# Where the first decay rows, the first block of k and its cast are queued in an attention-then-MLP kernel

## The chip, the cores and the metric

The kernel runs on one core of a Trainium2 chip. The metric is the device time of one execution in microseconds (us); the median of three runs of the kernel before is 340.68 us. The core has five engines that run their own instruction streams in order: TensorE (PE in the profile, its weight loads PEld), VectorE (DVE), ScalarE (ACT), GpSimd (POOL) and SyncE (SP), which here only issues transfers. ScalarE and GpSimd issue transfers as well. An engine waits for another through semaphores.

## The reference

Eight sequences of 576 positions with 8 heads of 64 go through causal attention with a decay: the scores get the difference of cumulated logarithms of a forget gate f. The result goes through an MLP of 512 to 2048 to 512 whose activation is h - tanh(h).

```python
scores = q @ k.T / sqrt(64)
cum = cumsum(log(clip(f, 1e-4, 1)))            # along the sequence
scores = where(causal, -1e9, scores + cum[i] - cum[j])
x = softmax(scores) @ v                        # heads side by side: 4608 x 512
h = x @ w_in                                   # 4608 x 2048
out = (h - tanh(h)) @ w_out                    # 4608 x 512
```

Inputs and output are float32. The kernel computes with 16-bit floats (f16) and sums in float32.

## The kernel before, in words

**Attention.** TensorE needs q and k with the head dimension on the partitions. For batch 0 they are loaded in five blocks of 128 positions (the last of 64) into `qa` and `ka`, with the positions on the partitions, 8 heads side by side and 68 columns a head. Columns 0 to 63 hold q or k; the others hold the decay, in such a way that one matmul over 67 rows gives score plus decay. A constant, -1 or 1, stands in the other side's column, so the columns are preset by memsets (L138 to L140). TensorE then turns each block by multiplying with an identity matrix `id16` (`quarter0`, L283, for four heads of q or of k; `trans0`, L297, for four heads of both, in one PSUM tile `t`), and VectorE or ScalarE copies the turned block into `QT` and `KT` (L286, L288, L308, L310). `half0` is `trans0` with both of its copies. `scores0` makes the scores of a block (L325, and L328 adds the causal mask), and ScalarE takes the exponential (L330). `values0` multiplies with v, `norm0` divides, `turn0` turns the result for the MLP.

**Decay.** The rows of f for all 64 heads lie in `lf` (a part of the tile `snap`) and are loaded in two parts, columns 0 to 255 and 256 to 575. `logs` clips each part on VectorE (L157) and takes the logarithm on ScalarE (L159). `decay_sum` cumulates on VectorE (L173); its first part is called only after both clips stand in VectorE's stream. `decay_turn` turns eight rows of the sums for batch 0 on TensorE into the PSUM tile `ct` (L192), and `decay_cols` writes them into the decay columns of `qa` and `ka` (L197 to L200).

**The first block of k.** k of block 0 is loaded as float32 by SyncE into `k0`, which borrows the space of the MLP's second weights (so the profile calls it `wout`, L124), and VectorE casts it into `ka` (L692). All the other loads of q, k, v and of the weights are issued by GpSimd, which casts them to f16 on the way (L94, L98, L105, L204, L208, L212). They use eight semaphores in turn, so from the ninth on GpSimd waits for the landing of the load eight places earlier before it issues the next.

**Order.** The order on every engine is the order of the program text; nothing is reordered. The head of the kernel is written out by hand: loads, then `spin(8)`, eight matmuls without use, then the decay sums, the turns and the scores of block 0, and so on. From batch 1 on, the work goes in slots: one slot holds the attention of two heads of one batch (`scores` L384, `values` L412, then a DMA turns the result, L427 and L429), with the loads for later batches and MLP steps put between by `slot`. How many MLP steps a slot takes stands in the list `TAKE`, whose first entry is for slot 4. What is left after the last slot runs at the end.

**MLP.** A step is about 0.9 us of TensorE: `mlp1` makes 512 columns of h (L474 for the first unit of 512 rows, L488 for the others), of which ScalarE takes the tanh (L440) and VectorE the difference (L441). For the first unit `mlp2` multiplies with the second weights (L609); the other units use a scheme with seven half-size products (`seven`, L529), for which VectorE adds up blocks (L455).

Of the kernel before, what the change touches and what calls it, by code (L numbers as in the profile page):

```python
# [8 lines left out]
FP32 = mybir.dt.float32  # L9
FP16 = mybir.dt.float16  # L10
# [12 lines left out]
def kernel(  # L23
# [10 lines left out]
    nc = tc.nc  # L34
    P = 128

    B, H, S, D = q.shape
# [5 lines left out]
    NJ = 5  # L43
    AW = D + 4
# [6 lines left out]
    UW = 512  # L51
# [13 lines left out]
    ps_tr = ctx.enter_context(tc.tile_pool(name="ps_tr", bufs=1, space=PSUM))  # L65
    ps_m = ctx.enter_context(tc.tile_pool(name="ps_m", bufs=3, space=PSUM))
# [10 lines left out]
    HH = H // 2  # L77
    raw = [[qkp.tile([P, RW], FP16, tag=f"{x}n{i}", name=f"{x}n{i}") for i in range(2)] for x in "qk"]
    qn, kn = ([t[0:S // NT6, :].rearrange("p (h n d) -> p h n d", h=H, n=NT6) for t in ts] for ts in raw)
    qa, ka = (t[0][:, 0:NJ * H * AW].rearrange("p (n h d) -> p n h d", n=NJ, h=H) for t in raw)  # L80
# [33 lines left out]
    def load_v(b, n):  # L114
# [5 lines left out]
    lf, cum = (x[0:NH, :] for x in snap)  # L120
    frows = f.rearrange("b h s -> (b h) s")
    nc.scalar.dma_start(out=lf[:, 0:2 * P], in_=frows[:, 0:2 * P])
    k0 = wout[:, 0:2, :].bitcast(FP32).rearrange("p a (h d) -> p (a h) d", d=D)
    nc.sync.dma_start(out=k0, in_=k[0, :, 0:P, :].rearrange("h p d -> p h d"))  # L124
    nc.scalar.dma_start(out=lf[:, 2 * P:S], in_=frows[:, 2 * P:S])
    id16 = cst.tile([P, P], FP16)
    id32 = cst.tile([H, H], FP32)
    neg16 = cst.tile([P, P], FP16)
# [6 lines left out]
    cq = cst.tile([NH, S], FP16)  # L135
    EL = [cst.tile([P, 192], FP16, tag=f"el{i}", name=f"el{i}") for i in range(3)]
    nc.vector.memset(one128, 1.0)
    nc.gpsimd.memset(qa[:, 0, :, D:AW], -1.0)  # L138
    nc.vector.memset(qa[:, 1:NJ, :, D:AW], -1.0)
    nc.vector.memset(ka[:, :, :, D + 2:AW], 1.0)  # L140
    nc.vector.memset(ones16, 1.0)
    nc.vector.memset(id16, 0.0)
# [5 lines left out]
    load_first(ka, k, 1)  # L148
    nc.gpsimd.affine_select(out=tri16, in_=tri16, compare_op=ALU.is_ge,
                            fill=BIG, base=0, pattern=[[1, P]], channel_multiplier=-1)  # L150
    nc.vector.memset(vn[0][:, :, :, D:VW], 1.0)
    nc.vector.memset(vn[0][D:P, NJ - 1, :, 0:D], 0.0)
    nc.vector.memset(KT[0][:, :, S:PITCH], 0.0)
# [18 lines left out]
    def decay_sum(c0, c1):  # L172
        nc.vector.tensor_tensor_scan(out=cum[:, c0:c1], data0=ones16[0:NH, c0:c1], data1=lf[:, c0:c1],  # L173
                                     initial=cum[:, c0 - 1:c0] if c0 else 0.0, op0=ALU.mult, op1=ALU.add)
# [12 lines left out]
    def decay_turn(blocks):  # L187
        if not CT:
            CT.append(ps_tr.tile([P, UW], FP32, tag="tr", name="ct"))
        for ib in blocks:  # L190
            t0 = min(ib * P, S - P)
            nc.tensor.transpose(out=CT[0][:, ib * H:(ib + 1) * H], in_=cum[0:H, t0:t0 + P], identity=id32)  # L192
# [38 lines left out]
    for b in range(2, B):  # L231
        p0 = (b - 1) * NPAIR
# [20 lines left out]
    def spin(n):  # L253
        av = ps_av.tile([P, 2, 512], FP32, tag="av", name="spin")
        for _ in range(n):
            nc.tensor.matmul(out=av[:, 0, :].rearrange("p (a n) -> p a n", n=P), lhsT=one128[:, 0, :],
                             rhs=one128.to_broadcast([P, UW // P, P]))
# [21 lines left out]
    def quarter0(ib, a, x, eng):  # L279
        t32 = ps_m.tile([P, UW], FP32, tag="m", name="t32")  # L280
        t16 = t32.bitcast(FP16)[0:D + 3, 0:HH * P].rearrange("p (h n) -> p h n", h=HH)
        for h in range(HH):
            nc.tensor.transpose(out=t16[:, h, :], in_=(qa, ka)[x][:, ib, a * HH + h, 0:D + 3], identity=id16)  # L283
        to = (QT, KT)[x][0][:, a * HH:(a + 1) * HH, ib * P:(ib + 1) * P]
        if eng == "A":
            nc.scalar.activation(out=to, in_=t16, func=AF.Copy)  # L286
        else:
            nc.vector.tensor_copy(out=to, in_=t16)  # L288

    def trans0(ib, a, pool, engs):  # L290
        p0 = max(0, (ib + 1) * P - S)
        pn = P - p0
        t32 = pool.tile([P, UW], FP32, tag="tr" if pool is ps_tr else "m", name="t32")
        t16 = t32.bitcast(FP16)[0:D + 3, 0:H * pn].rearrange("p (x h n) -> p x h n", x=2, h=HH)
        for x, src in enumerate((qa, ka)):
            for h in range(HH):
                nc.tensor.transpose(out=t16[:, x, h, :], in_=src[p0:P, ib, a * HH + h, 0:D + 3],  # L297
                                    identity=id16[p0:P, p0:P])
        T0[(ib, a)] = t16, engs

    T0 = {}

    def copy0(ib, a, x):
        w = min(P, S - ib * P)
        t16, engs = T0[(ib, a)]
        to = (QT, KT)[x][0][:, a * HH:(a + 1) * HH, ib * P:ib * P + w]
        if engs[x] == "A":
            nc.scalar.activation(out=to, in_=t16[:, x, :, :], func=AF.Copy)  # L308
        else:
            nc.vector.tensor_copy(out=to, in_=t16[:, x, :, :])  # L310

    def half0(ib, a, pool, engs):
        trans0(ib, a, pool, engs)
        copy0(ib, a, 0)
        copy0(ib, a, 1)
# [343 lines left out]
    def slot(p, take):  # L659
        items = att_items(p)  # L660
        whole, n, base = sum(c != "" for _, c in items), 0, goal[0]
        for i, (emit, what) in enumerate(items):
            emit()
            if take in FEW and p < 2 * NPAIR:
                if what in FEW[take] and not (what == "s1" and p > NPAIR) or what == "v":
                    step()
                continue
            n += what != ""
            upto(base + n * take // whole)
        goal[0] = base + take  # L670
        upto(goal[0])
# [17 lines left out]
    load_qk(kn, k, 1, 2, HH)  # L689
    spin(8)  # L690
    decay_sum(0, 2 * P)
    nc.vector.tensor_copy(out=ka[:, 0, :, 0:D], in_=k0)  # L692
    decay_turn((0, 1))
    decay_cols(0, 2)
    decay_sum(2 * P, S)
    nc.vector.tensor_scalar_mul(out=neg16, in0=id16, scalar1=-BIG)
    spin(1)
    quarter0(0, 0, 0, "V")
    quarter0(0, 0, 1, "A")
    half0(0, 1, ps_m, "VV")  # L700
    decay_turn((2, 3, 4))
    scores0(0, 0)
    decay_cols(2, NJ)
# [80 lines left out]
    norm0(4)  # L784
    step()
    goal[0] = done[0]
    TAKE = [4, 4, 5, 5, 7, 9] + [8, 8, 7, 8, 8, 7, 7] + 4 * [8, 8, 7, 7]
    for p in range(NPAIR, len(pairs) + 1):
        slot(p, TAKE[p - NPAIR])
        if p == NPAIR:  # L790
# [30 lines left out]
```

## Time and profile before

| | |
|---|---|
| median of three runs (340.52 to 342.07) | 340.68 us |
| the profiled execution, its own time | 341.17 us |
| span in its profile | 339.4 us |
| TensorE busy | 330.8 us, 97% |
| VectorE busy | 240.7 us, 71% |
| ScalarE busy | 227.2 us, 67% |
| GpSimd busy | 163.3 us, 48% |
| read from and written to memory | 36.85 and 9.44 MB |

The span runs from the program's first to its last instruction; the execution's own time is 1.8 us longer. A line of the profile that names an operation gives the engine, the line of the program, the tiles written and read (`out<-in`), the shape, and in brackets how long the engine was idle before it and what ended that. Matmuls are pipelined, so a TensorE that is shown as busy is not always at its peak.

### The profile page before, as it was taken

The numbers are of one execution on the slowest core, as the hardware profiler recorded it, in microseconds if no ns is written. First come the engines' busy times: TensorE is split into PE (matmuls) and PEld (weight loads), VectorE is DVE, ScalarE is ACT, GpSimd is POOL, SyncE is SP. The second block draws the span as 40 slices with busy tenths as digits, with TensorE's granted clock in tenths as the row PEclk, the third lists the DMA queues.
The fourth block names the chain that finished last, engine by engine and source line by source line (L and its number), as shares of the span: only waits on it lengthen the run. The fifth ranks groups of instructions, "written<-read, shape, count | busy, mean of one in ns | idle before, by whom it ended". The sixth has DMA issues, their size and how long they took to land.

```text
span 339.4 us, 8811 instructions
## 1 busy us (share of the span) xinstructions
PE 330.8 (97%) x3404; PEld 238.8 (70%) x3404; DVE 240.7 (71%) x491; ACT 227.2 (67%) x425; POOL 163.3 (48%) x324
## 2 busy tenths in 40 slices
PE   6999999999999999999999999999999999999995
PEld 3888876655588458888885578656877786486484
DVE  6688785649995886478845885588548874974973
ACT  4687887778856886588657875787568734624731
POOL 8958459851978627772776277633322210000000
PEclk9899999999999999999999999999999999999999
DMA  9999999999999999999999999998220022002002
GB/s 118 151 191 171 195 198 150 156 164 212 184 156 143 188 206 136 150 228 199 122 148 233 167 141 164 180 198 178 58 97 19 20 66 95 1 33 93 2 31 93
DMA packets 162955, 46.09 MB, mean 136 GB/s; under 512 B 141602, under 2 KB 162402, under 8 KB 162914
## 3 DMA queue, kind: packets, MB, share of 16 engines
q0 software_dynamic: 100208, 18.23, 81.6%
q1 hardware_dynamic: 62546, 27.17, 40.2%
q8 instruction: 26, 0.43, 0.5%
q10 hardware_dynamic: 160, 0.15, 0.1%
q14 instruction: 15, 0.12, 0.1%
HBM read 36.85 MB, written 9.44 MB: 136 GB/s over the span
## 4 chain that ended last, share of the span: by engine, by line
PE 90%; DVE 4%; ACT 3%; DMA 1%; issue 1%; ACTq 0%
PE hps L488 30%; PE cx L529 17%; PE cz L529 12%; PE ps L384 11%; PE av L412 7%; PE ops L609 4%; PE hps L474 3%; PE ps L325 2%; DVE gt L441 1%; PE t L297 1%; DMA snap<-in_f_dram 1%; PE av L340 1%; ACT e L330 1%; PE t L268 1%; ACT e L393 1%
## 5 line engine op out<-in xcount | busy, mean ns | idle before, releaser
L441 DVE TENSOR_TENSOR gt<-hps,th 128x512 f16<-128x512 f32 x144 | 98.8, 688 | 46.0 <-ACT th L440 45.2
L488 PE MATMUL hps<-XR,win 128*128 128x512 f16 (+4 forms) x640 | 125.7, 336 | 0.0
L393 ACT ACTIVATE e<-ps 128x512 f16<-128x512 f32 x168 | 98.3, 595 | 35.0 <-PE ps L384 30.9
L440 ACT ACTIVATE th<-hps 128x512 f32<-128x512 f32 x144 | 86.1, 598 | 27.8 <-PE hps L488 17.1
L403 POOL TENSOR_SCALAR_AFFINE_SELECT e<-e 128x128 f16<-128x128 f16 x162 | 57.3, 354 | 98.3 <-ACT e L393 97.9
L488 PEld LDWEIGHTS <-win 128*128 128x128 f16 x640 | 56.0, 97 | 43.3 <-issue 0.3
L384 PE MATMUL ps<-QT,KT 67*128 67x512 f16 (+1 forms) x336 | 68.3, 277 | 0.3 <-ACT e L393 0.3
L529 PEld LDWEIGHTS <-gt 128*128 128x128 f16 x640 | 60.5, 97 | 10.3 <-DVE gt L441 0.4
L384 PEld LDWEIGHTS <-KT 67*128 67x128 f16 x336 | 32.1, 98 | 18.4 <-issue 0.7
L94 POOL DMA_DIRECT2D vn<-in_v_dram x40 | 34.5, 863 | 5.7 <-DMA win<-in_moe_w_in_dram 3.1
L529 PE MATMUL cz<-wout,gt 128*128 128x256 f16 x256 | 32.4, 272 | 0.0
L412 PEld LDWEIGHTS <-e 128*128 128x128 f16 x784 | 27.9, 97 | 3.5
L412 PE MATMUL av<-vn,e 128*128 128x65 f16 x784 | 29.1, 193 | 0.0
L529 PEld LDWEIGHTS <-sw 128*128 128x128 f16 x256 | 23.7, 97 | 3.7
L522 DVE TENSOR_TENSOR snap<-cz,snap 128x512 f32<-128x512 f32 x24 | 16.5, 689 | 13.7 <-PE cz L529 6.0
L529 PE MATMUL cx<-kn,gt 128*128 128x256 f16 x192 | 25.2, 272 | 0.0
L420 DVE TENSOR_TENSOR xn<-av,rs 128x640 f16<-128x640 f32 x28 | 23.1, 825 | 1.0
L105 POOL DMA_DIRECT2D kn<-in_k_dram x25 | 21.3, 853 | 1.0 <-issue 1.0
L105 POOL DMA_DIRECT2D qn<-in_q_dram x25 | 21.3, 851 | 1.0 <-issue 1.0
L330 ACT ACTIVATE e<-ps 128x512 f16<-128x512 f32 x25 | 14.4, 595 | 4.3 <-PE ps L328 3.0
L474 PE MATMUL hps<-XR,win 128*128 128x256 f16 x128 | 16.6, 272 | 0.3 <-DVE gt L441 0.3
L566 ACT ACTIVATE snap<-cx 128x512 f32<-128x512 f32 (+1 forms) x18 | 9.9, 550 | 10.4 <-PE cx L529 10.4
(114 smaller groups left out, 377.3 us busy)
## 6 DMA issues: line engine op xcount, KB each, us to landing
vn<-in_v_dram POOLq DMA_DIRECT2D x32, 128.0 KB, 6.9
out_dram<-snap SPq DMA_DIRECT2D x16, 256.0 KB
qn<-in_q_dram POOLq DMA_DIRECT2D x24, 128.0 KB, 6.8
kn<-in_k_dram POOLq DMA_DIRECT2D x23, 128.0 KB, 5.1
QT<-TQ SPq DMA_DIRECT2D x10, 288.0 KB
KT<-TK SPq DMA_DIRECT2D x10, 288.0 KB
out_dram<-ost SPq DMA_DIRECT2D x11, 256.0 KB
win<-in_moe_w_in_dram POOLq DMA_DIRECT2D x4, 512.0 KB, 8.8
```

What stands on the lines that cost most here:

```text
L94: nc.gpsimd.dma_start(out=dst[0:pn, n, h0:h1, 0:D], in_=src[b, h0:h1, n * P:n * P + pn, :].rearrange("h p d -> p h d"))
L105: nc.gpsimd.dma_start(out=to, in_=src[b, :, n * P:n * P + pn, :].rearrange("h p d -> p h d"))
L384: nc.tensor.matmul(out=ps[:, col:col + n], lhsT=KT[b % 2][0:D + 3, h, j * P:(j + 1) * P], rhs=QT[b % 2][0:D + 3, h, i0:i0 + n], start=True ...
L393: nc.scalar.activation(out=e[:, lo:hi], in_=ps[:, lo:hi], func=AF.Exp, scale=qscale)
L403: nc.gpsimd.affine_select(out=view, in_=view, compare_op=ALU.is_ge, fill=0.0, base=0, pattern=pat, channel_multiplier=-1)
L412: nc.tensor.matmul(out=av[:, a, ib, :], lhsT=E.pop((b, 2 * c + a, j, ib)), rhs=vn[b % 2][:, j, 2 * c + a, 0:D + 1], start=(j == 0), stop=( ...
L420: nc.vector.tensor_tensor(out=xn.rearrange("p i (a d) -> p a i d", a=2), in0=av[:, :, :, 0:D], in1=rs.to_broadcast([P, 2, NJ, D]), op=ALU. ...
L440: nc.scalar.activation(out=th, in_=hps, func=AF.Tanh, scale=-1.0)
L441: nc.vector.tensor_tensor(out=to, in0=view(hps), in1=view(th), op=ALU.add)
L474: nc.tensor.matmul(out=hps[:, w * SB:(w + 1) * SB], lhsT=win[:, ci, ft * P:(ft + 1) * P], rhs=XR[:, ci, t * SB:(t + 1) * SB], start=(ci == ...
L488: nc.tensor.matmul(out=hps[:, o:o + n], lhsT=win[:, ci, ft * P:(ft + 1) * P], rhs=XR[:, ci, t:t + n], start=(ci == 0), stop=(ci == NCH - 1))
L529: nc.tensor.matmul(out=ps, lhsT=stationary(u, LHS[ph], ft, m), rhs=moving(RHS[ph], ft), start=fresh and ft == 0, stop=(ft == HF - 1), skip ...
```

## The change

Four things are moved:

- The second part of the decay rows is issued by SyncE, as its first transfer, and not by ScalarE behind the first part. The float32 k of block 0 follows it on SyncE.
- The cast of that k runs on GpSimd, behind the third load and the second mask, and ahead of the loads of block 2. VectorE no longer does it. In exchange VectorE presets all of q's extra columns, block 0's included.
- `trans0` can turn q alone or k alone. In block 0, the second half of q is turned directly behind the first half of q, and then come the two halves of k. The copies are the same.
- Slot 14 takes seven MLP steps and not eight; each later step runs one place later, and one more runs at the end.

```diff
     nc.scalar.dma_start(out=lf[:, 0:2 * P], in_=frows[:, 0:2 * P])
     k0 = wout[:, 0:2, :].bitcast(FP32).rearrange("p a (h d) -> p (a h) d", d=D)
+    nc.sync.dma_start(out=lf[:, 2 * P:S], in_=frows[:, 2 * P:S])
     nc.sync.dma_start(out=k0, in_=k[0, :, 0:P, :].rearrange("h p d -> p h d"))
-    nc.scalar.dma_start(out=lf[:, 2 * P:S], in_=frows[:, 2 * P:S])
...
-    nc.gpsimd.memset(qa[:, 0, :, D:AW], -1.0)
-    nc.vector.memset(qa[:, 1:NJ, :, D:AW], -1.0)
+    nc.vector.memset(qa[:, :, :, D:AW], -1.0)
...
     nc.gpsimd.affine_select(out=tri16, in_=tri16, compare_op=ALU.is_ge,
                             fill=BIG, base=0, pattern=[[1, P]], channel_multiplier=-1)
+    nc.gpsimd.tensor_copy(out=ka[:, 0, :, 0:D], in_=k0)
...
-    def trans0(ib, a, pool, engs):
+    def trans0(ib, a, pool, engs, xs=(0, 1)):
         p0 = max(0, (ib + 1) * P - S)
         pn = P - p0
...
-        for x, src in enumerate((qa, ka)):
+        if 0 in xs:
+            t32 = pool.tile([P, UW], FP32, tag="tr" if pool is ps_tr else "m", name="t32")
+            t16 = t32.bitcast(FP16)[0:D + 3, 0:H * pn].rearrange("p (x h n) -> p x h n", x=2, h=HH)
+            T0[(ib, a)] = t16, engs
+        t16 = T0[(ib, a)][0]
+        for x in xs:
...
     decay_sum(0, 2 * P)
-    nc.vector.tensor_copy(out=ka[:, 0, :, 0:D], in_=k0)
     decay_turn((0, 1))
...
     quarter0(0, 0, 0, "V")
+    trans0(0, 1, ps_m, "VV", (0,))
     quarter0(0, 0, 1, "A")
-    half0(0, 1, ps_m, "VV")
+    trans0(0, 1, ps_m, "VV", (1,))
+    copy0(0, 1, 0)
+    copy0(0, 1, 1)
...
-    TAKE = [4, 4, 5, 5, 7, 9] + [8, 8, 7, 8, 8, 7, 7] + 4 * [8, 8, 7, 7]
+    TAKE = [4, 4, 5, 5, 7, 9] + [8, 8, 7, 8, 7, 7, 7] + 4 * [8, 8, 7, 7]
```

More of the change, by code (lines that the diff above doesn't have):

```diff
@@ L288, in quarter0 @@
             nc.vector.tensor_copy(out=to, in_=t16)
-    def trans0(ib, a, pool, engs):
+    def trans0(ib, a, pool, engs, xs=(0, 1)):
         p0 = max(0, (ib + 1) * P - S)
         pn = P - p0
-        t32 = pool.tile([P, UW], FP32, tag="tr" if pool is ps_tr else "m", name="t32")
-        t16 = t32.bitcast(FP16)[0:D + 3, 0:H * pn].rearrange("p (x h n) -> p x h n", x=2, h=HH)
-        for x, src in enumerate((qa, ka)):
+        if 0 in xs:
[4 more added lines that the diff above has]
+        for x in xs:
             for h in range(HH):
-                nc.tensor.transpose(out=t16[:, x, h, :], in_=src[p0:P, ib, a * HH + h, 0:D + 3],
+                nc.tensor.transpose(out=t16[:, x, h, :], in_=(qa, ka)[x][p0:P, ib, a * HH + h, 0:D + 3],
                                     identity=id16[p0:P, p0:P])
-        T0[(ib, a)] = t16, engs
     T0 = {}
```

## The prediction

> **What bounds the kernel now.** I read the page's busy times first, then the busy time by stage, then who waited for whom on TensorE, then the chain of work over the first 12 us, and last the engines' own timelines there.
>
> ```profile
> PE 330.8 (97%) x3404; PEld 238.8 (70%) x3404; DVE 240.7 (71%) x491; ACT 227.2 (67%) x425; POOL 163.3 (48%) x324
> ...
> 100.00:150.00 50.00, 50.00 (x525) 36.76 (x523) 33.77 (x68) 34.41 (x67) 33.03 (x63) 1.00 1.71 173
> ...
> PE ct L192 <- DVE snap L173: 2.1, 1, 2.1
> ...
> PE ps L325 <- ACT e L330: 1.0, 3, 0.4
> ```
>
> The stage rows (stretch, its length, then PE, PEld, DVE, ACT, POOL busy, clock, DMA) show TensorE busy in all of a stretch of 50 us at full clock, and the page in 97% of the span. The longest of its few waits, 2.1 us, is for the sum of the decay rows. So whatever makes TensorE's first turns start earlier is carried to the end, unless something later is not ready for an earlier TensorE.
>
> ```profile
> 0.82 0.55 ACTq L122
> 1.40 3.79 DMA snap<-in_f_dram
> 5.21 0.58 DVE snap L157
> 5.86 0.60 DVE snap L173
> 6.51 0.29 PE ct L192 x2
> 6.79 0.32 PE spin L256
> 7.16 0.94 PE t L283 x8
> 8.10 0.85 PE t L297 x8
> 8.95 0.42 PE ct L192 x3
> ```
>
> This chain (start, length, what) says what holds the first turns: the second part of the decay rows (columns 256 to 575) is issued behind the first on ScalarE, lands at 5.19, and VectorE clips it (L157) before it may do the first sum (L173).
>
> **The change part by part.**
>
> ```profile
> 0.82 0.55 ACTq L122 DMA_DIRECT2D snap<-in_f_dram  x1
> 1.40 0.61 ACTq L125 DMA_DIRECT2D snap<-in_f_dram  x1
> 4.65 0.42 ACT L159 ACTIVATE snap<-snap 64x256 f32<-64x256 f32 x1 [1.32 <-DVE snap L157]
> ...
> 4.21 0.40 DVE L157 TENSOR_SCALAR snap<-snap 64x256 f32<-64x256 f32 x1 [1.32 <-DMA snap<-in_f_dram]
> 5.21 0.58 DVE L157 TENSOR_SCALAR snap<-snap 64x320 f32<-64x320 f32 x1 [0.60 <-DMA snap<-in_f_dram]
> ...
> 6.38 0.39 DVE L692 CAST kn<-wout 128x512 f16<-128x512 f32 x1
> 6.83 0.23 DVE L197 TENSOR_SCALAR qn<-ct 128x16 f16<-128x16 f32 x1
> ```
>
> *Second decay rows on SyncE, first.* They are issued at about 0.82 instead of 1.40. The first rows took 0.82 to 4.21, 3.4 us; the second 1.40 to 5.19, 3.8 us. Issued at 0.82 they land between 4.2 and 4.6. VectorE is then in its first clip, which ends at 4.21 + 0.40 = 4.61, so the second starts at 4.61 instead of 5.21: **-0.60 us**, the idle time in its row. Ends: 0, if they land at 5.2 all the same; -0.9, if both land sooner because the 256 KB of k no longer moves beside the first. I take -0.60, since the rows' own durations give it. The first logarithm (4.65 to 5.07) is no obstacle: the first sum can start near 5.25. ScalarE loses an issue of 0.61 and then waits for VectorE as before (1.32 in its row): 0.
>
> The first turns also need q of block 0:
>
> ```profile
> 1.37 1.90 POOL L98 DMA_DIRECT2D qn<-in_q_dram  x2 [0.43 <-issue]
> ...
> qn<-in_q_dram POOLq DMA_DIRECT2D x2, 128.0 KB, 4.5
> ```
>
> Issued at 1.37 and some 4.5 us to landing, it is there at 5.9, 0.65 before the new start of the turns, 7.16 - 0.60 = 6.55. It is a floor: more than 1.2 us cannot be gained here.
>
> *The cast leaves VectorE.* It ran 6.38 to 6.77, and the next instruction waited for TensorE's turns of the sums (6.51 + 0.29 = 6.80): gain 0.03, taken as 0. If the turns came 0.4 us sooner it would have been worth 0.4.
>
> *The cast on GpSimd.* The page has no GpSimd copy; its nearest groups are these.
>
> ```profile
> L403 POOL TENSOR_SCALAR_AFFINE_SELECT e<-e 128x128 f16<-128x128 f16 x108 | 32.9, 305 | 46.6 <-ACT e L393 46.3
> L403 POOL TENSOR_SCALAR_AFFINE_SELECT e<-e 128x256 f16<-128x256 f16 x54 | 24.4, 452 | 51.7 <-ACT e L393 51.6
> ...
> L763 POOL MEMSET qn<- 32x576 f16 x1 | 0.6, 573 | 0.0
> ...
> 4.49 0.32 POOL L149 TENSOR_SCALAR_AFFINE_SELECT tri<-tri 128x128 f16<-128x128 f16 x1
> 4.74 0.90 POOL L98 DMA_DIRECT2D qn<-in_q_dram  x1
> ...
> 0.82 0.45 SPq L124 DMA_DIRECT2D wout<-in_k_dram  x1
> ```
>
> A memset of 576 elements takes 573 ns, so 512 some 0.52 us; the selects grow by (452 - 305)/128 = 1.15 ns an element, so 512 some 305 + 384 x 1.15 = 0.75 us. The ends are 0.52 and 0.75, and I take 0.65. It waits for the float32 k, now issued behind an issue of 0.61, at 1.43 instead of 0.82; with the 3.8 us of the larger decay transfer it lands at 5.2. Ends: 4.9 (3.4 us) and 6.0, if the q loads of GpSimd's queue slow it. So the cast ends at 5.2 + 0.65 = 5.9 (5.4 to 6.8). The turns of k that need it come after eight turns of q from 6.55, not before 7.15: **0**, covered by 1.2 us of other turns.
>
> Beside it runs the first sum on VectorE, about 5.25 to 5.9, which reads two operands from SBUF. How such an instruction fares beside GpSimd:
>
> ```profile
> L455 DVE TENSOR_TENSOR sw<-gt x32: 412/416/654, 80.6 to 324.8; 128x512 f16<-128x512 f16 x32
> L455 DVE TENSOR_TENSOR gt<-gt x32: 411/418/518, 95.8 to 328.1; 128x512 f16<-128x512 f16 x32
> ```
>
> (Columns: least, median, longest ns.) Undisturbed it takes 0.41 us, at worst 0.65. So the sum may lose 0 to 0.24 us, on the path; the median being the undisturbed time, I take **+0.10**.
>
> The Trainium skill, GPSIMD Engine Reference, section 8 (Key points), says that GpSimd shares its SBUF interfaces with VectorE and contends with instructions that have two SBUF inputs, which speaks against putting a cast beside this sum. The long ones of these rows agree; by the rule as it stands the full 0.24 us would be paid and the sum would be 0.14 us worse.
>
> *What is queued behind the cast.* GpSimd issues its loads in order, and the third q load waited for nothing at 4.74. Now it stands behind the cast, at 5.9: **+1.2 us for every later load** (0.7 to 2.1). The memset that leaves GpSimd's queue ahead of the first loads lets them start a little sooner, and the rest is swallowed by the same wait. Whether TensorE notices depends on the slack of each load.
>
> ```profile
> 20.31 0.91 POOL L94 DMA_DIRECT2D vn<-in_v_dram  x1 [2.40 <-DMA win<-in_moe_w_in_dram]
> ...
> 23.56 1.03 PE L474 MATMUL hps<-XR,win 128*128 128x256 f16 x8
> ...
> 36.12 0.71 POOL L212 DMA_DIRECT2D qn<-in_q_dram  x1
> ...
> qn<-in_q_dram POOLq DMA_DIRECT2D x1, 288.0 KB, 18.4
> ...
> 56.42 0.42 PE L268 MATMUL t<-id,qn 96*128 96x96 f16 x6
> ```
>
> From 20 us on GpSimd itself waits for landings, so the transfers are limited by their rate, and a hole of 1.2 us at 5 us is carried along. The first weights, whose wait ended at 20.31, are needed at 23.56: over 3 us of slack. The tightest that I found is q of batch 2: issued at 36.12, landed 18.4 later at 54.5, needed at 56.42: 1.9 us. With the loads 1.2 later and TensorE 0.5 earlier, 0.2 is left. That costs nothing, but it **caps any gain at 1.9 - 1.2 = 0.7 us** (1.2 down to below 0).
>
> *The memset of q's extra columns* grows by a quarter on VectorE, which then idles until 4.21: 0.
>
> *q turned whole ahead of k.*
>
> ```profile
> 8.14 0.59 ACT L286 ACTIVATE KT<-t 67x512 f16<-67x512 f16 x1 [0.33 <-PE t L283]
> ...
> 8.15 0.41 DVE L288 COPY QT<-t 67x512 f16<-67x512 f16 x1
> ```
>
> The same sixteen turns, about 0.11 us each in the chain above. ScalarE's copy of the first k half comes four turns later, VectorE's copy of the second q half four sooner. Before, TensorE was busy without a break from 7.16 to 9.37 (8.95 + 0.42), 0.6 us longer than ScalarE's copy lasted (8.73), and the copies hid behind it; four turns later (0.45) it would end 0.2 before. Without that cover the first scores would wait for it, 0.59 at most. I take 0 (-0.2, where VectorE's earlier copy helps, to +0.3, half of the copy).
>
> *Seven steps in slot 14.* Slot 14 runs from 116.5 to 125.7.
>
> ```profile
> 116.50:125.70 9.20, 9.20 (x75) 4.88 (x74) 7.95 (x16) 7.87 (x16) 2.28 (x7) 1.00 1.49 216
> ```
>
> TensorE is busy in all of it, so there is no wait to remove. The moved step is an mlp1 step of unit 2: four 128x512 matmuls, one tanh, one gate, no sums and no DMA. Every later step and its stores come one step later relative to the attention work; the stores meet the turns of x in SP's queue one step later, and the tail has one step more. TensorE's work is the same, and it waits for neither: 0 (-0.1 to +0.2).
>
> **The sum** against the profiled execution's own 341.17 (span 339.4 and 1.8 around it): -0.60 + 0.10 = -0.5, so 340.7. That execution is 0.5 above the median of the runs, 340.68; against the median the forecast is **340.2**.
>
> **The rivals.**
>
> *The clock stays full (faster).*
>
> ```profile
> 3.94:7.36 3.42, 1.27 (x9) 0.52 (x7) 2.45 (x9) 1.93 (x3) 3.42 (x6) 1.00 1.96 126
> 7.36:10.77 3.41, 3.41 (x34) 3.15 (x32) 2.49 (x9) 1.43 (x4) 3.41 (x6) 0.50 2.12 135
> ```
>
> After a stretch in which TensorE was busy 1.27 of 3.42 us, the next 3.41 us ran at half clock. With the turns 0.6 earlier the share rises from 37% to about 55%. If that is enough, the second stretch runs at full clock. It would save at most half of 3.41, 1.7 us; VectorE's 2.49 us there leaves 0.9. With the 0.6 that is -1.5: 339.2, or 340.0 if the cap of 0.7 holds; with the far ends (-0.9 - 1.7), 338.1. For it: full stretches keep the clock. Against: the threshold is unknown between 37% and 100%, and the cap.
>
> The Trainium skill, TensorE: Matmul & The Clock Gate, Part 1, has the clock fall only after a window of about 3.4 us without work. The rows disagree, since a gap of about 2 us sufficed here. By its rule neither gap would throttle, and this rival would be worth nothing.
>
> *The rows land no earlier.* The change then doesn't do what it says: 3.8 us is the queue's pace and the 80 KB decide. 0 + 0.1: 340.8.
>
> *The cast comes late (slower).* k's transfer meets GpSimd's q loads and lands late. The place is q of batch 2 at 56.42: a cast that ends at 4.74 + 1.9 = 6.6 takes the whole gain, and each us beyond costs one. Over 0.5% (1.7 us) it is from a cast that ends at 8.3 on; there the first k turns wait too, at 7.15. One that ends at 8.4 gives 342.5. For it: the cast stands in the same queue as all loads. Against: in the rows the transfers issued before 1.5 us took 3.4 and 3.8 us, so 8.3 would need twice that.
>
> **How the numbers follow.** Forecast 0.52, full clock 0.19, rows no earlier 0.13, late cast 0.16. The forecast's own range is 339.8 to 340.8 (0.9 gained at most by the rows, 0.24 of contention and 0.3 of copies lost). The range, 338.8 to 341.7, takes in the full clock but its far end and the mild half of the late cast. What a measurement can tell from no change is about 0.5%, 1.7 us: faster needs under 339.0, which part of the full clock gives (0.15); slower, over 342.4, the worse part of the late cast and what I don't see (0.13); the same 0.72.
>
> **What would show it.** Right: the second L157 starts directly behind the first, near 4.6; the first `ct` near 5.9; GpSimd's copy 0.5 to 0.8 us long, ending before 6.6, with TensorE's k turns not waiting for it; the third q load issued near 5.9; the turns of batch 2's q not waiting; slot 14 as busy as before. Wrong: a wait of TensorE for `qn` or `kn` near 56 us, for GpSimd near 7 us, a first sum far over 0.67 us, or a half-clock stretch that is gone or has moved.

## The result, and the profile after

The changed kernel is slower: 343.16 us median (340.78 to 350.74) beside 341.18 us of the kernel before, a ratio of **1.0055, with a 95% interval of 1.0028 to 1.0082**. The forecast was 340.2 and a range up to 341.7. The ratio leaves out executions more than 1.5% above the fastest; of the changed kernel's 22 those are three, and nine lie over 344.5 us, so its mean, 343.98 beside 341.56, is worse than its median tells.

The profiled execution took 343.20 us, span 341.5. First the page's busy times and the waits of TensorE (who waited for what: us in all, times, longest), as they are after the change.

```profile
PE 332.6 (97%) x3404; PEld 240.2 (70%) x3404; DVE 240.1 (70%) x490; ACT 227.3 (67%) x425; POOL 163.1 (48%) x324
...
PE t L283 <- DMA qn<-in_q_dram: 1.7, 1, 1.7
...
PE ps L386 <- DMA KT<-TK: 0.5, 1, 0.5
PE ps L386 <- issue: 0.4, 1, 0.4
```

The wait of 2.1 us for the decay sums is gone. In its place stands one of 1.7 us for q, and there are two that the profile before did not have, both at the first scores of a batch (L386 is the old L384; `issue` means that the profile names no cause). Where the head went shows in the timelines of VectorE, GpSimd and TensorE (start, length, what; in brackets the idle time before, and what ended it):

```profile
3.22 0.64 DVE L157 TENSOR_SCALAR snap<-snap 64x256 f32<-64x256 f32 x2 [0.30 <-DMA snap<-in_f_dram]
...
3.99 0.68 DVE L173 TENSOR_TENSOR_SCAN snap<-ones,snap 64x256 f32<-64x256 f16 x1
...
4.53 0.30 POOL L148 TENSOR_SCALAR_AFFINE_SELECT tri<-tri 128x128 f16<-128x128 f16 x1
6.63 0.61 POOL L150 CAST kn<-wout 128x512 f16<-128x512 f32 x1 [1.79 <-DMA wout<-in_k_dram]
7.18 0.90 POOL L98 DMA_DIRECT2D qn<-in_q_dram  x1
...
4.73 0.29 PE L192 MATMUL ct<-id,snap 8*128 8x8 f32 x2
4.95 0.39 PE L256 MATMUL spin<-one 128*128 128x512 f16 x1
7.03 0.38 PE L283 MATMUL t<-id,qn 128*67 128x128 f16 x4 [1.69 <-DMA qn<-in_q_dram]
```

Both clips are done by 3.9 and the sums are turned at 4.73, against 6.51 before. But the float32 k is not there until 6.6, GpSimd stands idle for 1.79 us before its cast, the third q load is issued at 7.18 instead of 4.74, and q of block 0 is late as well: the first turns start at 7.03, a mere 0.13 sooner than before.

The second loss is later, where batches 4 and 6 begin (slots 16 and 24). First the two places before, then after the change:

```profile
134.15 0.60 PE L384 MATMUL ps<-QT,KT 67*128 67x512 f16 x3
...
204.79 0.60 PE L384 MATMUL ps<-QT,KT 67*128 67x512 f16 x3
```

```profile
134.67 0.38 PE L386 MATMUL ps<-QT,KT 67*128 67x512 f16 x1 [0.37 <-issue]
...
205.97 0.58 PE L386 MATMUL ps<-QT,KT 67*128 67x512 f16 x2 [0.51 <-DMA KT<-TK]
```

Both waits end with k's copies: by the completion marks in the trace the copy for slot 16 landed at 134.58 and the one for slot 24 at 205.92.

And the clock (stretch, length, busy times of PE, PEld, DVE, ACT, POOL, then the granted clock):

```profile
4.38:7.79 3.41, 1.61 (x18) 1.08 (x18) 2.00 (x7) 1.49 (x2) 1.61 (x4) 1.00 1.85 131
7.79:11.20 3.41, 3.41 (x34) 3.22 (x32) 1.80 (x7) 1.46 (x3) 3.41 (x5) 0.50 1.07 68
11.20:14.61 3.41, 3.37 (x33) 3.20 (x31) 1.38 (x3) 2.39 (x5) 3.41 (x5) 0.50 2.21 141
```

Two stretches of half clock follow the gap, where the profile before had one. The first scores of slot 4 start 0.83 us later (before, then after):

```profile
32.37 0.38 PE L384 MATMUL ps<-QT,KT 67*128 67x512 f16 x1
```

```profile
33.20 0.38 PE L386 MATMUL ps<-QT,KT 67*128 67x512 f16 x1
```

From there to the end of the span it is 307.1 us before and 308.3 after. These 1.2 us lie at the two new waits: 0.88 of them is idle time, and the rest lies in the 4 us ahead of them. The two parts, 0.83 and 1.2, make up the 2.1 us by which the spans differ. They are read from one execution on either side; whether the 0.83 belongs to the change is a question for the runs below.

### The profile page after: what moved, and what is told of

The parts are those of the page before. It is cut to its first block, busy times and chain, and to the rows that moved or that the text cites. A ratio compares the mean times of both kernels' runs of the same rounds, so it can differ in the third digit from the quotient of the medians.

```text
span 341.5 us, 8812 instructions
## 1 busy us (share of the span) xinstructions
PE 332.6 (97%) x3404; PEld 240.2 (70%) x3404; DVE 240.1 (70%) x490; ACT 227.3 (67%) x425; POOL 163.1 (48%) x324
## 4 chain that ended last, share of the span: by engine, by line
PE 83%; DVE 6%; ACT 4%; DMA 3%; issue 1%; SPq 0%; ACTq 0%; POOLq 0%
PE hps L490 26%; PE cx L531 16%; PE cz L531 12%; PE ps L386 9%; PE av L414 6%; PE ops L611 4%; DVE gt L443 3%; PE hps L476 3%; PE ps L327 2%; DMA KT<-TK 2%; DMA qn<-in_q_dram 2%; ACT th L442 1%; PE t L300 1%; ACT e L395 1%; PE av L342 1%
## 5 line engine op out<-in xcount | busy, mean ns | idle before, releaser
L442 ACT ACTIVATE th<-hps 128x512 f32<-128x512 f32 x144 | 86.2, 598 | 32.8 <-PE hps L490 26.1
L405 POOL TENSOR_SCALAR_AFFINE_SELECT e<-e 128x128 f16<-128x128 f16 x162 | 55.3, 342 | 100.4 <-ACT e L395 99.9
L386 PE MATMUL ps<-QT,KT 67*128 67x512 f16 (+1 forms) x336 | 68.1, 277 | 1.2 <-DMA KT<-TK 0.5
L386 PEld LDWEIGHTS <-KT 67*128 67x128 f16 x336 | 31.9, 98 | 20.5 <-issue 1.4
L531 PE MATMUL cz<-wout,gt 128*128 128x256 f16 x256 | 32.4, 272 | 0.0
```

The source lines that it names most:

```text
L386: nc.tensor.matmul(out=ps[:, col:col + n], lhsT=KT[b % 2][0:D + 3, h, j * P:(j + 1) * P], rhs=QT[b % 2][0:D + 3, h, i0:i0 + n], start=True ...
L405: nc.gpsimd.affine_select(out=view, in_=view, compare_op=ALU.is_ge, fill=0.0, base=0, pattern=pat, channel_multiplier=-1)
L442: nc.scalar.activation(out=th, in_=hps, func=AF.Tanh, scale=-1.0)
L531: nc.tensor.matmul(out=ps, lhsT=stationary(u, LHS[ph], ft, m), rhs=moving(RHS[ph], ft), start=fresh and ft == 0, stop=(ft == HF - 1), skip ...
```

## The experiments

Two theories were set against each other. **A**, k's copies: from batch 3 on, k reaches TensorE through a transposing transfer and two copies in SP's queue (`place`, `KT<-TK`), which go at the transfers' pace. Taking a step out of slot 14 brings the attention 0.84 us sooner against them (slot 14 lasts 8.36 us instead of 9.20; the expectations say 0.87). **B**, the head: the late float32 k, the late q and the clock are all of it. By the completion marks in the trace before, the copy for slot 16 had landed at 132.7 and the one for slot 24 at 203.9, while their first scores started at 134.15 and 204.79: a slack of 1.5 and 0.85 us.

**Slot 14 alone** (`s14_alone`), on the kernel before:

```diff
-    TAKE = [4, 4, 5, 5, 7, 9] + [8, 8, 7, 8, 8, 7, 7] + 4 * [8, 8, 7, 7]
+    TAKE = [4, 4, 5, 5, 7, 9] + [8, 8, 7, 8, 7, 7, 7] + 4 * [8, 8, 7, 7]
```

> The kernel before with seven steps in slot 14 alone. Theory A (k's copies): the attention of slot 16 and later comes one step, 0.87 us, sooner against copies of k (KT<-TK) that go at the transfers' pace. Their slack in the profile before is 1.5 us at slot 16 and 0.85 us at slot 24 (landings at 132.7 and 203.9, first scores at 134.15 and 204.79), so waits of 0 to 0.4 us in a calm execution, more where transfers are late: ratio 1.001 to 1.004, with waits for KT<-TK at the first scores of a batch. Theory B (head): the loss comes from the head alone: 0.999 to 1.001 and no such wait.

Ratio 1.0018 (0.9993 to 1.0043), median 341.91. The interval takes in both theories and no change at all: no verdict. Its profiled execution had no wait for k's copies. Its head was late, with the first scores of slot 4 at 34.25; even so the copy for slot 24 landed at 205.78, only 0.05 us ahead of its scores at 205.83.

**The change without slot 14** (`s14_undone`):

```diff
-    TAKE = [4, 4, 5, 5, 7, 9] + [8, 8, 7, 8, 7, 7, 7] + 4 * [8, 8, 7, 7]
+    TAKE = [4, 4, 5, 5, 7, 9] + [8, 8, 7, 8, 8, 7, 7] + 4 * [8, 8, 7, 7]
```

> The changed kernel with eight steps in slot 14 again. Theory A: about half of the loss stays, the 0.8 us of the head, and the waits at slots 16 and 24 (0.37 and 0.51 us in the changed kernel's profile) are gone: ratio 1.001 to 1.003. Theory B: the loss stays whole, 1.004 to 1.007. If the head's delay eats the copies' slack as well, waits for KT<-TK remain even here.

Ratio 1.0018 (0.9990 to 1.0046), median 341.94, mean 341.99 against the whole change's 343.98; one execution of 12 over 344.5. No wait at slots 16 or 24. This speaks for A, though the interval reaches into B's range, and neither this kernel nor slot 14 alone is clear of no change. The clock of its head, and where slot 4 then started (row of TensorE's timeline):

```profile
7.72:11.14 3.42, 3.24 (x33) 3.15 (x32) 1.93 (x7) 1.46 (x3) 3.42 (x5) 0.50 1.22 78
11.14:14.00 2.86, 2.38 (x42) 2.26 (x41) 1.45 (x5) 2.21 (x5) 2.86 (x4) 1.00 2.24 143
...
31.82 0.38 PE L386 MATMUL ps<-QT,KT 67*128 67x512 f16 x1
```

With one stretch of half clock, as the profiled execution before had, the same new head brings slot 4 0.55 us sooner (31.82 against 32.37), close to the 0.5 of the forecast; with two, it was 0.83 later. The second stretch does not come from the new transfers: `cast_alone` below, whose transfers are the old ones, has two as well, and its slot 4 starts at 33.30.

**Nine steps in slot 14** (`s14_nine`), on the kernel before:

```diff
-    TAKE = [4, 4, 5, 5, 7, 9] + [8, 8, 7, 8, 8, 7, 7] + 4 * [8, 8, 7, 7]
+    TAKE = [4, 4, 5, 5, 7, 9] + [8, 8, 7, 8, 9, 7, 7] + 4 * [8, 8, 7, 7]
```

> The kernel before with nine steps in slot 14: the attention of slot 16 and later comes one step later against the copies of k. Theory A: their slack grows by 0.87 us, so executions in which the copies are late wait less: ratio 0.996 to 1.000 and less spread. Theory B: 0.999 to 1.001.

Ratio 1.0031 (1.0005 to 1.0058): slower, which neither theory said. The wait it shows is another one:

```profile
PE hps L488 <- DMA XR<-xn: 1.2, 2, 1.0
```

With the attention a step later, the MLP asks for the turned result of batch 3 (`XR`) before it is there. Slot 14 thus stands between two transfers of the same queue: with one more step the turned results are late, with one fewer the slack of k's copies is gone, and in the whole change they are late.

**The cast behind block 2's loads** (`cast_later`), the change with eight steps in slot 14:

```diff
-    nc.gpsimd.tensor_copy(out=ka[:, 0, :, 0:D], in_=k0)
     nc.vector.memset(vn[0][:, :, :, D:VW], 1.0)
...
     load_first(ka, k, 2)
+    nc.gpsimd.tensor_copy(out=ka[:, 0, :, 0:D], in_=k0)
     load_v(0, 0)
```

> The changed kernel with eight steps in slot 14 and with GpSimd's cast put behind the two loads of block 2. If the loads that stood behind the waiting cast are what the head lost, the third q load is issued near 4.7 again, the hole in the transfers at 8 to 9 us is gone, and the ratio is 0.997 to 1.000. If the head's loss is k's and q's transfers running beside each other (q of block 0 landing at 6.9), the first turns still wait until 7.0 and the ratio is that of the kernel with slot 14 undone.

Ratio 1.0003 (0.9980 to 1.0026). The loads of block 2 are issued at 4.99 and 5.88 again, and the cast, at 6.75, waits for nothing. The first turns still wait for q, until 6.89. So the loads behind the cast were not a loss that can be seen beside q's own lateness.

**k's copies sooner** (`k_copies_sooner`): the whole change, with the copies ahead of the turn of x in SP's queue. It takes away what they wait for.

```diff
-            at(p0 + 2, (0 if near else 5) + a, lambda b=b, a=a: place(KT, TK, b, a))
+            at(p0 + 2, a, lambda b=b, a=a: place(KT, TK, b, a))
```

> The whole change, with one thing more: in SP's queue the two copies of k (KT<-TK) of each batch from 4 on go ahead of the turn of x of the pair before, which they stood behind. It takes away what makes the first scores of slots 16 and 24 wait. Theory A (the copies of k come late, because the head starts the loads later and slot 14 brings the attention sooner): no wait for KT<-TK at the first scores, the executions of 344.5 us and more that were 9 of 22 in the changed kernel become 1 or 2 of 12, median 341.5 to 342.5, ratio 1.000 to 1.003. Theory B (all of it is the head): the copies' place is of no use, median 343 to 344, ratio 1.004 to 1.007. If the turn of x, now behind, is what the MLP waits for, a wait for XR<-xn stands in the profile and the ratio stays above 1.004.

Ratio 1.0019 (0.9995 to 1.0043), median 341.95, one execution of 12 over 344.5. The copy for slot 16 lands at 132.2, 1.8 us ahead of its scores, and no wait for `KT<-TK` or `XR<-xn` is left; a short one for k of batch 2 is (0.3 us, at 58.5). With slot 14 still at seven steps, the ratio is that of `s14_undone`, as theory A had it; by the interval a rest of 0.4% can't be told from none.

**The rows alone** (`rows_alone`), on the kernel before: the second decay rows first on SyncE, the cast still on VectorE.

```diff
+    nc.sync.dma_start(out=lf[:, 2 * P:S], in_=frows[:, 2 * P:S])
     nc.sync.dma_start(out=k0, in_=k[0, :, 0:P, :].rearrange("h p d -> p h d"))
-    nc.scalar.dma_start(out=lf[:, 2 * P:S], in_=frows[:, 2 * P:S])
```

> The kernel before with the second decay rows on SyncE first and the float32 k behind them; the cast stays on VectorE. If the float32 k lands late because it now runs beside GpSimd's q loads, the rows land near 3.5 as in the changed kernel, but the cast on VectorE waits for k until about 6.5, ahead of the decay columns, and the first turns start near 7.2 as before or later: ratio 1.000 to 1.003. If k's lateness belongs to GpSimd's cast, k lands near 5.2 and the first turns start near 6: ratio 0.996 to 0.999.

Ratio 1.0017 (0.9994 to 1.0039). The sums are turned at 5.04, and then everything stands behind the late k on VectorE:

```profile
6.83 0.43 DVE L692 CAST kn<-wout 128x512 f16<-128x512 f32 x1 [1.85 <-DMA wout<-in_k_dram]
7.17 0.22 DVE L197 TENSOR_SCALAR qn<-ct 128x16 f16<-128x16 f32 x1
...
7.50 0.40 PE L283 MATMUL t<-id,qn 128*67 128x128 f16 x2 [1.54 <-DVE kn L199]
```

So k's lateness comes from the order of the transfers and not from GpSimd's cast.

**The cast alone** (`cast_alone`), on the kernel before: the cast on GpSimd, all transfers as before.

```diff
     nc.gpsimd.affine_select(out=tri16, in_=tri16, compare_op=ALU.is_ge,
                             fill=BIG, base=0, pattern=[[1, P]], channel_multiplier=-1)
+    nc.gpsimd.tensor_copy(out=ka[:, 0, :, 0:D], in_=k0)
...
-    nc.vector.tensor_copy(out=ka[:, 0, :, 0:D], in_=k0)
```

> The kernel before with the cast of block 0's k moved from VectorE to GpSimd, at the changed kernel's place, and all transfers issued as before. If the cast hurts by waiting for a late k: here k lands at 4.5 as before, GpSimd's cast runs from about 4.8 to 5.4, the third q load is issued near 5.4 and not 7.2, and the ratio is 0.999 to 1.001. If a cast in GpSimd's queue hurts whatever k does: 1.001 to 1.004.

Ratio 1.0008 (0.9986 to 1.0030), as expected. k is there when GpSimd comes to it:

```profile
4.75 0.64 POOL L151 CAST kn<-wout 128x512 f16<-128x512 f32 x1
5.30 0.91 POOL L98 DMA_DIRECT2D qn<-in_q_dram  x1
```

**Thirteen matmuls without use** (`spin_13`), on the kernel before:

```diff
-    spin(8)
+    spin(13)
```

> The kernel before with thirteen instead of eight matmuls without use at the start, which cover TensorE's idle 2.1 us before the decay sums come. If the spread of the executions comes in part from where the clock's stretches of 3.4 us fall on that gap, the half-clock stretch behind it is gone or rarer, the first scores of slot 4 start at 31 to 32 and not at 32.4 to 34.3, and the ratio is 0.995 to 0.999 with less spread. If the clock's state is not set by that gap: 0.999 to 1.001.

Ratio **0.9972** (0.9945 to 0.9999), median 340.10 against 341.20. It is the one kernel of the record whose interval lies below 1, and only just. The stretches that were half empty and at half clock before:

```profile
3.94:7.36 3.42, 3.38 (x13) 1.24 (x12) 2.72 (x9) 1.94 (x3) 3.42 (x6) 1.00 1.93 126
7.36:10.77 3.41, 3.38 (x54) 3.01 (x53) 3.12 (x11) 2.32 (x6) 3.41 (x6) 1.00 2.15 137
...
31.04 0.38 PE L384 MATMUL ps<-QT,KT 67*128 67x512 f16 x1
```

TensorE makes 54 matmuls in the second one, where it made 34, and slot 4 starts 1.33 us sooner than in the profile before, though the first turns start no sooner. (The trace's first clock record is at 6.23. The 1.00 of the first line covers time without a record as well: the thirteen took 5.48 us, 0.42 each, where six of that size take 1.46 us at full clock in `s14_nine`, 0.24 each.) From 6.23 on the clock is full. All three profiles with more matmuls without use (this one and the last two kernels below) have the full clock for the rest of the head from 5.9 to 7.1 on; the eleven others, some of them after one full stretch near 4 us, have it only from 10.3 to 15.8 on.

**The change once more** (`after_again`), with no edit, beside the next three kernels.

> The changed kernel once more, beside the next three on one chip. Theory A+B (head and slot 14 together use up the slack of k's copies): a ratio of 1.003 to 1.008 again, several executions over 344.5, float32 k landing after 5.5 and the cast behind it, and a wait of the first scores of a later batch for KT<-TK, if the profiled execution is not one of the calm ones. If the loss was an accident of the chip it ran on: 0.999 to 1.002.

Ratio 1.0025 (0.9997 to 1.0053), median 342.31, mean 343.87, four executions of 12 over 344.5. The interval takes in no change, so the ratio alone does not repeat the loss; the mean does. Together with the first comparison 13 of 34 executions of the change lie over 344.5, against 3 of 36 of `s14_undone`, `cast_later` and `k_copies_sooner`. The profiled execution, one of the calmer ones at 342.23, waits 0.38 us at slot 16, until k's copy lands at 134.28.

**Six steps in slot 14** (`after_six`), the change with double the dose:

```diff
-    TAKE = [4, 4, 5, 5, 7, 9] + [8, 8, 7, 8, 7, 7, 7] + 4 * [8, 8, 7, 7]
+    TAKE = [4, 4, 5, 5, 7, 9] + [8, 8, 7, 8, 6, 7, 7] + 4 * [8, 8, 7, 7]
```

> The changed kernel with six steps in slot 14, double the dose. Theory A: the attention from slot 16 on comes another 0.87 us sooner against k's copies, so the first scores of slot 16 wait 0.9 us longer than in the changed kernel beside it (some 1.2 us), and the ratio is 0.002 to 0.003 higher. If slot 14 is neutral: the ratio of the changed kernel beside it, within 0.001.

Ratio 1.0133 (1.0085 to 1.0181), median 348.73: theory A's sign, and four times its size. The profiled execution (349.91) shows what makes it so large.

```profile
133.76:137.54 3.78, 0.00 (x1) 0.03 (x1) 1.36 (x3) 0.00 (x0) 0.29 (x1) 0.87 1.43 176
136.56:143.39 6.83, 5.85 (x49) 4.39 (x50) 1.38 (x4) 1.09 (x2) 2.33 (x4) 0.50 1.24 157
...
131.22 1.27 SPq L112 DMA_DIRECT2D KT<-TK  x2
...
137.54 1.01 PE L386 MATMUL ps<-QT,KT 67*128 67x512 f16 x3 [3.78 <-issue]
```

The copies are issued at 131.2, 2.5 us later than in the changed kernel (128.75): k's transposing transfer ahead of them in SP's queue was issued 0.8 us later and held the queue for 7.06 us instead of 5.76. They land at 137.45 by the completion marks. TensorE waits 3.78 us, and 6.83 us at half clock begin within the wait. TensorE is busy for 5.85 us of these, which costs up to half of it, 2.9 more. So this long wait was paid nearly twice; the waits of 0.37 and 0.51 in the changed kernel brought no half clock. The changed kernel's executions of 345 to 351 us may be of this kind, but none of them was profiled.

**Both repairs of the head** (`cast_later_spin`): `cast_later`, and six matmuls without use instead of one between the turns of the sums and those of q.

```diff
-    spin(1)
+    spin(6)
```

> The changed kernel with eight steps in slot 14, the cast behind the loads of block 2, and six instead of one matmuls without use between the turns of the decay sums and those of q, which cover TensorE's wait for q's load. If the clock's stretches make the difference, the first turns start near 6.5 to 6.9 with no half-clock stretch behind, slot 4 starts at 31 and the ratio is 0.995 to 0.999; if q's late load alone sets it: 1.000 to 1.001, as without them.

Ratio 1.0006 (0.9980 to 1.0032), median 341.00: as without them. In the profiled execution q landed so late that its turns started at 7.62. The clock was full from 5.9 on all the same, and slot 4 started at 31.56; then slot 24 waited 0.6 us for k's copies, with eight steps in slot 14. An earlier head alone can use up that slack.

**Thirteen matmuls and k's copies sooner** (`spin_13_k_sooner`), on the kernel before: the edits of `spin_13` and of `k_copies_sooner`.

> The kernel before with thirteen matmuls without use and with k's copies ahead of the turn of x in SP's queue. If late copies of k are behind the slow executions of the kernel before as well, the spread above the median shrinks against the thirteen alone (two of 12 over 343): 0.994 to 0.998. If the turn of x is what is then late: waits for XR<-xn and 0.998 to 1.002.

Ratio 0.9997 (0.9966 to 1.0028), median 340.12 against 341.00. Eight of 12 lie at 340.3 or below and the others at 342 to 344.4. Its profiled execution waits for neither transfer. The copies' place brings nothing to the kernel before that shows, and the gain of the thirteen, which is in this kernel too, is not confirmed by the ratio, though the median is again 0.9 us lower.

## Why the prediction was wrong

**Slot 14, taken as 0 (-0.1 to +0.2): the step that failed.** Slot 14's own row was read: TensorE was busy in all of it, so nothing could be gained, and the work stayed the same. But for the loads of the head the question was put the other way, what is then not ready for an earlier TensorE, and it was never put for the slots behind slot 14, where taking out a step makes the attention 0.84 us earlier. The slack was there to read, 1.5 us at slot 16 and 0.85 at slot 24. In the whole change the profile has waits of 0.37 and 0.51 that cost 1.2 us, with six steps one of 3.78, and with the copies ahead of what they stood behind, or with eight steps in `s14_undone`, none. The slack that mattered lay after 60 us, and the search had stopped at 56. That the copies are what is late is shown; that they make up most of the 0.55% is not, since the intervals with and without them overlap. Slot 14 by itself fits the 0 that was forecast: behind slot 4 the profile of `s14_alone` is as long as the one before, 307.1 us.

**The second decay rows, taken as -0.60.** The mechanism was right and the size too small: the first part landed at about 3.2 and the second at 3.5, and the turns of the sums came 1.8 us sooner. The far end was given as -0.9. How much of it reached the turns of q hung on the next term.

**The floor, q of block 0 at 5.9.** It was named, with 0.65 us to spare, and it was taken as fixed. It is not: q landed at 6.9 here, 6.1 to 7.5 in the others with this order of transfers, and in this profile that took back all but 0.13 us of the rows' gain. Where q landed by 6.4 (`after_again`, `after_six`, `s14_undone`, `k_copies_sooner`), the turns started 0.6 to 0.9 us sooner than before, about what was forecast.

**The float32 k, taken to land at 5.2 (4.9 to 6.0).** By the completion marks it landed at 5.8 to 7.2 in the profiles with the new order (6.57 in this one), and at 4.3 to 4.5 with the old. The packets of SP's queue show it, first before and then after the change, over 1.5 to 4 us of the span (packets, MB, share of 16 engines):

```profile
q1 hardware_dynamic: 1040, 0.26, 46.2%
```

```profile
q1 hardware_dynamic: 631, 0.22, 37.4%
```

Issued first, all of k's 0.26 MB is in the first line, when GpSimd's queue had moved 0.01 MB. Issued 0.65 us later, behind decay rows of 0.08 MB, some 0.14 of its 0.26 MB is, and the rest moves beside GpSimd's q loads; both are late. The 3.8 us taken from the decay rows was a fair measure of k by itself, 3.7 us before the change. What it left out is the q loads, and the far end of 6.0 was too near.

The Trainium skill, DMA: Bandwidth & Descriptors, section "Issuing engines are not separate DMA queues", says that transfers of ScalarE, SyncE and GpSimd run on the same 16 engines and interleave. These rows agree. The rule gives no size; it speaks for the far end of the range, and k landed past that.

**GpSimd's cast.** Its 0.61 us lies by the 0.65 taken. The contention with the first sum, +0.10, did not come up: the sum (0.68 us, 0.67 before) was over long before the cast began. Where a sum and the cast did meet, in `k_copies_sooner`, it was the cast that lost:

```profile
5.51 0.87 DVE L173 TENSOR_TENSOR_SCAN snap<-ones,snap,snap 64x320 f32<-64x320 f16 x1
6.31 0.53 DVE L697 TENSOR_SCALAR neg<-id 128x128 f16<-128x128 f16 x1
...
5.87 0.92 POOL L150 CAST kn<-wout 128x512 f16<-128x512 f32 x1 [1.09 <-DMA wout<-in_k_dram]
```

The second sum took the 0.87 us that it took before, the cast 0.92 instead of 0.61 (1.07 in `after_again`, where TensorE then waited 0.2 for it). The operation behind the sum (L697) took 0.53 beside the cast, against 0.16 in the changed kernel, where they did not meet.

**The loads behind the cast, a hole that is carried along.** The third q load was 2.4 us later instead of 1.2, past the 1.9 at which the cap was set. But the hole shrank on the way: q of batch 2 landed 1.1 us later than before, at 55.6, and was needed at 57.3. In `s14_undone`, with the third q load 1.9 later, it landed 0.4 us sooner than before. So the cap of 0.7 and the price of one us for each us were wrong too, without harm here. The one trace with a wait near the place, 0.3 us for k of batch 2 at 58.5, is that of `k_copies_sooner`.

**q turned whole ahead of k, taken as 0 (-0.2 to +0.3).** In `s14_undone` and `cast_later_spin` the first scores wait 0.2 us for ScalarE's copy of k, within the range; in the other profiles with the new order nothing of the kind shows. No run has this part alone.

**The late cast as the way to a slower kernel.** A cast that ends after 6.6 should take the whole gain; it ended at 7.24. But the loss of 1.9 us is not shown to lie there: `cast_later` and `s14_undone` leave at most 0.3 and 0.5% for the whole head, and both intervals take in 0.

**The clock as the way to a faster one.** The gap of TensorE's work stayed in the wrong stretch. The share of work there rose from 37 to 47%, not to 55, and two stretches at half clock followed where this rival had none. Nor does 55% look like enough: in `after_again` and `s14_undone` the share was 59 and 61%, and half clock followed as well. That filling the gap is worth something was right: with `spin_13`, whose profile has no half clock after 6.23, slot 4 starts 1.33 us sooner than in the profile before, within the 0.9 to 1.7 that were worked out. This is one execution on either side.

**Open.** How the loss divides between head and slot 14 is not known: each alone is 1.0018 with an interval of a quarter of a per cent to either side, which takes in 1, and together they are 1.0055 and 1.0025. That the new head loses anything is not shown. Up to slot 4, `before`, `s14_alone` and `s14_nine` are one program, and their slot 4 starts at 32.4, 34.3 and 32.8 us; the changed kernel, `after_again`, `after_six`, `k_copies_sooner` and `s14_undone` are another, with 33.2, 32.9, 31.9, 32.6 and 31.8. So the 0.83 us between the first two profiles is chance as far as these show. Why the copies land later against slot 14 when both parts are there (17.2 us after the slot's start in both profiles of the change, 16.1 with the head alone and 15.1 with the seven steps alone, one execution each) was not found.

## What to carry to other kernels

An edit that removes work from a full engine makes everything behind it earlier; for each later stage, look up when its inputs landed and take the smallest slack as the cap, to the end of the program and not only near the edit. A transfer moved behind a small one can lose more than the small one's issue time when another queue's transfers begin in between: here 2.1 us for an issue 0.65 later. A short stretch of work without use that covers a gap of TensorE is worth a try beside closing the gap: here the half clock ended by 7.1 us in all three profiles that had it, while the ratio of one kernel was just clear of 1 and those of the other two were not.

## What the runs showed of the hardware that was not expected

- A busy stretch did not always bring the full clock back. In the changed kernel TensorE was busy 3.41 of 3.41 us from 7.79 to 11.20 at half clock, and the next 3.41 us ran at half clock as well; before, and in `s14_undone`, one stretch of 3.4 us was enough. The Trainium skill, TensorE: Matmul & The Clock Gate, Part 1, has the full clock after at least one busy stretch of about 3.4 us; here it took two, and in `cast_alone` and `after_again` as well. Many of the matmuls in these stretches are turns; whether those count like the others, no run shows.
- A stretch that was more than half busy still brought half clock behind it. In `after_again` TensorE was busy 2.01 of 3.41 us:

```profile
4.10:7.51 3.41, 2.01 (x20) 1.18 (x19) 2.91 (x8) 1.98 (x4) 2.46 (x4) 1.00 1.93 136
7.51:14.34 6.83, 6.78 (x64) 6.41 (x62) 3.09 (x9) 3.95 (x7) 6.83 (x9) 0.50 1.59 101
```

- In `after_six` a single wait of 3.78 us, after more than 120 us at full clock, came with 6.83 us at half clock.
- The clock column reads 1.00 where the trace has no record yet. In `s14_alone` the first record is at 15.81, and TensorE's pace ahead of it is that of half clock: 48 matmuls of the head in 5 us, and 35 in the 2.2 us behind it.

```profile
10.77:15.81 5.04, 5.00 (x48) 4.83 (x47) 1.80 (x4) 3.34 (x6) 5.04 (x7) 1.00 2.03 146
15.81:18.00 2.19, 1.81 (x35) 1.69 (x34) 1.85 (x7) 1.26 (x4) 2.11 (x4) 1.00 1.42 185
```

- Executions of one program differ by where these stretches fall on the head: the first scores of slot 4 start at 32.37 us in the profile before and at 34.25 in that of `s14_alone`, which is the same up to there. That is as much as the whole loss of 1.9 us.
- Behind slot 4 there is next to no such spread. In the eight profiles without a new wait there, from slot 4's first scores to the end of the span it is 307.0 to 307.1 us each time. So the time of a profiled execution is where its slot 4 starts, plus its waits for transfers behind that.
